# Nystrom attention and two feed-forward layers on one core: GpSimd's subtractions issued in halves

## The chip, the cores and the metric

One core of a Trainium2 chip runs the whole program in one launch. The metric is the device time of that launch in microseconds, the median of several runs. Engines have short names in the profile: PE is TensorE (PEld its weight loads), DVE is VectorE, ACT is ScalarE, POOL is GpSimd, SP is SyncE.

## The reference

Three stages follow each other. Attention with 32 landmarks for 4 batches of 8 heads, 576 positions and 64 channels; a feed-forward layer with the activation h * cos(h); and a second one with a leaky ramp whose slope is learned per channel:

```python
q_lm = q.reshape(B, H, m, S // m, D).mean(axis=3)
k_lm = k.reshape(B, H, m, S // m, D).mean(axis=3)
A, Bm, C = sm(q, k_lm), sm(q_lm, k_lm), sm(q_lm, k)
Z = Bm.transpose(0, 1, 3, 2) / (norm1(Bm) * norminf(Bm) + 1e-06)
for _ in range(6):
    Z = 2 * Z - Z @ Bm @ Z
x = A @ Z @ C @ v                      # to [2304, 512]
h = x @ w_in;  x = (h * np.cos(h)) @ w_out
h = x @ w_in;  out = (np.maximum(h, 0) + alpha * np.minimum(h, 0)) @ w_out
```

`sm` is the scaled softmax. Both layers have 2304 rows, width 512 and inner width 2048. Everything is float32.

## The kernel before, in words

Products in float32 are made of three products in a rounded format. An operand x is split into a high part, `hi = round(x)`, made by ScalarE (`AF.Copy` into a rounded tile), and a low part, `lo = x - hi`, made by a subtraction. A product is then hi*hi + hi*lo + lo*hi, three matmuls into the same PSUM bank. So each operand of each large product passes one subtraction, and the matmuls that read the low part are the last of their three.

The subtractions go through one helper, `sub` (line 413), which issues one `tensor_tensor` on the engine that it is given. Its name stands at line 414 in the profile, whatever it was called for. It is called

- for the low part of a tick's activation, 288 columns (`tick`, L1076 of the source);
- for the low parts of weights and of the second layer's inputs, 256 or 512 columns (`split`, `hl`, `half`, `t_make`, `y_load`), of the attention's rows, 576 columns, and of the second layer's activations (`btick`, `form`);
- for the differences that Strassen's scheme for the second layer needs, 256 columns (`diff_`, `t_make`);
- for subtracting the maximum in the attention's softmax, 18 groups of 32 columns.

The program is recorded first, as operations with their buffers. Then an order written out by hand, the string `ORDER`, says in which order all of them are issued, and where a name ends in `/V` or `/A` also on which engine. An operation that names GpSimd first runs there if the order says nothing else. 200 subtractions run on GpSimd, the others on VectorE. Each engine takes its own instructions in the order in which they are issued; semaphores that are placed by the framework hold an instruction until the data that it reads are written and the buffer that it writes is free. The framework follows this by the range of columns.

Stages, by the profile's time: to about 40 us the attention of the first batch and the conversion of weights; then 128 ticks of the first layer (`tick`) to about 420 us, into which the attention of the other batches is woven; then the second layer (`btick` and, in Strassen's form, `mtick` with `narrow`) to the end. A tick is: six matmuls into a PSUM bank `h` (L1063), a rounding on ScalarE (L1068), a reduction on VectorE that reads PSUM (L1070), a sine on ScalarE (L1072), a product on VectorE that reads PSUM (L1073), the high part on ScalarE (L1075), the low part (L414), and twelve matmuls into four banks `acc` (L1088). Beside the ticks VectorE converts weights with integer operations on 512 columns (L570, L572, L574). L1425 and L1469 are the second layer's first products, L1620 and L1738 its second ones; L409 and L411 copy banks, L1448 and L1481 add them up.

Of the kernel before, what the change touches and what calls it, by code (L numbers as in the profile page):

```python
# [13 lines left out]
ALU = mybir.AluOpType  # L14
# [335 lines left out]
def kernel(  # L350
# [54 lines left out]
    ENG = {"DVE": nc.vector, "POOL": nc.gpsimd}  # L405
# [5 lines left out]
            ENG[e].tensor_copy(o, i)  # L411

    def sub(e, o, a, b):
        ENG[e].tensor_tensor(o, a, b, op=ALU.subtract)  # L414

    ps = ctx.enter_context(tc.tile_pool(name="ps", bufs=2, space=bass.MemoryType.PSUM))
    dram = ctx.enter_context(tc.tile_pool(name="dram", bufs=1, space=bass.MemoryType.DRAM))
# [66 lines left out]
    op = g.op  # L484
# [68 lines left out]
    def split(f, sl, n, hi, lo, target=None, after=(), vec=True):  # L553
        op(act(n), lambda e: nc.scalar.activation(hi.t[:, 0:n], sl(f.t), AF.Copy), r=[f], w=[hi, lo], target=target,
           after=after)
        op([pool(n), dve(n)] if vec else pool(n),
           lambda e: sub(e, lo.t[:, 0:n], sl(f.t), f32(hi.t[:, 0:n])), r=[f, hi], w=[lo], target=target)
# [68 lines left out]
    def unit(u, tu, ta=None):  # L626
# [231 lines left out]
        for ch in range(2):  # L858
# [5 lines left out]
            if m == 0 and ch == 0:  # L864
# [3 lines left out]
               r=[sa[ch]], w=[at])  # L868
        op(dve(S), lambda e, mxa=mxa, at=at: nc.vector.reduce_max(mxa.t, at.t, axis=AX.X), r=[at], w=[mxa])
        op(tt, lambda e, mxa=mxa, at=at: sub(e, at.t, at.t, mxa.t.to_broadcast([P, NBK, M])), r=[mxa], rw=[at])  # L870
        op(act(S), lambda e, at=at: nc.scalar.activation(at.t, at.t, AF.Exp), rw=[at], aset="exp")
        op(dve(S), lambda e, sma=sma, at=at: nc.vector.reduce_sum(sma.t, at.t, axis=AX.X), r=[at], w=[sma])
# [174 lines left out]
    def tick(s):  # L1047
# [9 lines left out]
        def h1_mm(e):  # L1057
# [16 lines left out]
           target=T + 2.6)  # L1074
        op(act(CW), lambda e: nc.scalar.activation(gh.t, hc.t, AF.Copy), r=[hc], w=[gh, gl])  # L1075
        op([pool(CW), dve(CW)], lambda e: sub(e, gl.t, hc.t, f32(gh.t)), r=[hc, gh], w=[gl])  # L1076
        jg = JG if b < 2 else NF
        ja, jb = j // jg * jg, j // jg * jg + jg - 1
# [730 lines left out]
```

## Time and profile before

| | us |
|---|---|
| runs, median (lowest to highest) | 798.35 (797.6 to 801.91) |
| profiled execution, its own time | 795.35 |
| span of its instructions | 793.5 |
| TensorE busy | 776.8 |
| VectorE busy | 640.2 |
| ScalarE busy | 437.6 |
| GpSimd busy | 240.0 |

The span runs from the first to the last instruction; 1.85 us of the execution's time lie around it. Busy time is the union of an engine's instructions; the granted clock is the share of TensorE's 2.4 GHz that the chip gave. A row of a timeline gives start, length, engine, line, operation, what is written from what, how many instructions it merges, and in brackets the idle time of the engine before it and who ended it. Where several instructions are merged, the length is that of all.

### The profile page before, as it was taken

The numbers are of one execution on the slowest core, as the hardware profiler recorded it, in microseconds if no ns is written. First come the engines' busy times: TensorE is split into PE (matmuls) and PEld (weight loads), VectorE is DVE, ScalarE is ACT, GpSimd is POOL, SyncE is SP. The second block draws the span as 40 slices with busy tenths as digits, with TensorE's granted clock in tenths as the row PEclk, the third lists the DMA queues.
The fourth block names the chain that finished last, engine by engine and source line by source line (L and its number), as shares of the span: only waits on it lengthen the run. The fifth ranks groups of instructions, "written<-read, shape, count | busy, mean of one in ns | idle before, by whom it ended". The sixth has DMA issues, their size and how long they took to land. (4 is left out here: it accounts for less than half of the span.)

```text
span 793.5 us, 18121 instructions
## 1 busy us (share of the span) xinstructions
PE 776.8 (98%) x6906; PEld 714.2 (90%) x6906; DVE 640.2 (81%) x1374; ACT 437.6 (55%) x992; POOL 240.0 (30%) x257
## 2 busy tenths in 40 slices
PE   8989999999999999999999999999999999999997
PEld 6577899998988999999998898889889999999997
DVE  4999988788988879888669797676977689776886
ACT  5487666778765555666755343233455475555431
POOL 0334232777323222343534342145311011000200
PEclk9999999999999999999999999999999999999999
DMA  9993447998877657774567854767166514563450
GB/s 284 246 301 129 123 148 170 195 213 175 267 238 250 221 161 261 243 246 135 202 202 269 290 172 158 239 238 266 43 202 227 208 68 139 181 207 125 136 197 28
DMA packets 114278, 154.80 MB, mean 195 GB/s; under 512 B 55568, under 2 KB 73488, under 8 KB 114192
## 3 DMA queue, kind: packets, MB, share of 16 engines
q1 hardware_dynamic: 114032, 153.39, 62.8%
q8 instruction: 54, 0.88, 0.5%
q14 instruction: 32, 0.26, 0.1%
q10 hardware_dynamic: 160, 0.26, 0.1%
HBM read 114.57 MB, written 39.06 MB: 194 GB/s over the span
## 5 line engine op out<-in xcount | busy, mean ns | idle before, releaser
L414 POOL TENSOR_TENSOR m<-m,m 128x288 fp32r<-128x288 f32 (+4 forms) x176 | 176.2, 1014 | 441.3 <-ACT m L1075 138.5
L1088 PE MATMUL acc<-m,m 128*128 128x288 f32 x1536 | 230.9, 298 | 0.0
L1088 PEld LDWEIGHTS acc<-m,m 128*128 128x128 f32 x1536 | 210.6, 188 | 15.3 <-issue 11.9
L414 DVE TENSOR_TENSOR m<-m,m 128x512 fp32r<-128x512 f32 (+5 forms) x268 | 151.9, 587 | 26.5 <-ACT m L1573 12.3
L1063 PE MATMUL h<-m,m 128*128 128x288 f32 x768 | 124.2, 299 | 1.2 <-DVE m L1073 0.7
L1063 PEld LDWEIGHTS h<-m,m 128*128 128x128 f32 x768 | 107.6, 188 | 6.6 <-DVE m L1073 3.8
L1738 PE MATMUL acc<-m,m 128*128 128x512 f32 x384 | 97.3, 394 | 0.0
L1072 ACT ACTIVATE m<-m,quarter 128x288 f32<-128x288 f32 x128 | 67.8, 535 | 44.1 <-DVE m L1070 43.2
L1469 PE MATMUL x<-m,m 128*128 128x256 f32 x588 | 85.6, 286 | 1.8 <-DVE m L414 0.8
L1469 PEld LDWEIGHTS x<-m,m 128*128 128x128 f32 x588 | 75.4, 189 | 4.7 <-ACT m L409 1.4
L1738 PEld LDWEIGHTS acc<-m,m 128*128 128x128 f32 x384 | 68.6, 188 | 11.9
L1073 DVE TENSOR_TENSOR m<-m,h 128x288 f32<-128x288 f32 x128 | 57.0, 449 | 25.6 <-ACT m L1072 20.4
L1573 ACT ACTIVATE m<-m 128x256 fp32r<-128x256 f32 (+2 forms) x96 | 45.8, 508 | 54.1 <-DVE m L1587 21.7
L1068 ACT ACTIVATE m<-h 128x288 int32<-128x288 f32 x128 | 51.5, 404 | 34.5 <-PE h L1063 32.7
L1070 DVE SCALAR_TENSOR_TENSOR m<-h,m 128x288 f32<-128x288 f32 x128 | 57.5, 450 | 15.6 <-ACT m L1068 14.6
L1075 ACT ACTIVATE m<-m 128x288 fp32r<-128x288 f32 x128 | 55.3, 439 | 26.4 <-DVE m L1073 19.8
L1620 PE MATMUL acc<-m,m 128*128 128x256 f32 x485 | 69.0, 281 | 0.1
L1620 PEld LDWEIGHTS acc<-m,m 128*128 128x128 f32 x485 | 62.3, 189 | 0.5 <-ACT m L1573 0.3
L409 ACT ACTIVATE m<-x 128x256 f32<-128x256 f32 (+5 forms) x75 | 29.3, 398 | 38.4 <-PE x L1469 28.6
L574 DVE SCALAR_TENSOR_TENSOR m<-m,m 128x512 int32<-128x512 int32 x64 | 46.7, 734 | 0.3
L572 DVE SCALAR_TENSOR_TENSOR m<-m,m 128x512 int32<-128x512 int32 x64 | 45.3, 711 | 0.3
L1425 PE MATMUL h<-m,m 128*128 128x256 f32 x300 | 43.0, 283 | 0.8 <-ACT m L409 0.8
(176 smaller groups left out, 1121.7 us busy)
## 6 DMA issues: line engine op xcount, KB each, us to landing
m<-wf2d SPq DMA_DIRECT2D x72, 512.0 KB, 4.7
m<-in_moe_w_in_dram SPq DMA_DIRECT2D x32, 512.0 KB, 5.3
m<-in_moe_w_out_dram SPq DMA_DIRECT2D x32, 512.0 KB, 5.5
wf2d<-m SPq DMA_DIRECT2D x28, 512.0 KB, 4.7
m<-w1d SPq DMA_DIRECT2D x32, 256.0 KB, 5.2
m<-wo2d SPq DMA_DIRECT2D x32, 256.0 KB, 3.3
y1d<-m SPq DMA_DIRECT2D x24, 288.0 KB, 4.7
m<-wi2d SPq DMA_DIRECT2D x20, 256.0 KB, 3.8
```

Of the source, the lines that this page charges most:

```text
L414: ENG[e].tensor_tensor(o, a, b, op=ALU.subtract)
L574: op(dve(512), lambda e: nc.vector.scalar_tensor_tensor(cf.t, rv(0), 29, cf.t, op0=ALU.logical_shift_right, op1=ALU.bitwise_or), r=[raw], ...
L1063: nc.tensor.matmul(out=hp.t[:, 0:CW], lhsT=w_[:, js], rhs=x[:, cs], start=(i == 0), stop=(i == 5))
L1068: op(act(CW, True), lambda e: nc.scalar.activation(k_.t, hp.t[:, 0:CW], AF.Copy, scale=INV2PI, bias=0.25), r=[hp], w=[k_], target=T + 0.8)
L1070: op(dve(CW), lambda e: nc.vector.scalar_tensor_tensor(u.t, hp.t[:, 0:CW], INV2PI, k_.t, op0=ALU.mult, op1=ALU.subtract), r=[hp, k_], w=[u])
L1072: op(act(CW), lambda e: nc.scalar.activation(u.t, u.t, AF.Sin, scale=2.0 * math.pi, bias=quarter), rw=[u], aset="sin")
L1073: op(dve(CW), lambda e: nc.vector.tensor_tensor(hc.t, u.t, hp.t[:, 0:CW], op=ALU.mult), r=[hp, u], w=[hc], target=T + 2.6)
L1075: op(act(CW), lambda e: nc.scalar.activation(gh.t, hc.t, AF.Copy), r=[hc], w=[gh, gl])
L1088: nc.tensor.matmul(out=yg[o].t[:, 0:CW], lhsT=w_.t[:, sl], rhs=x.t, start=(j == ja and i == 0), stop=(j == jb and i == 2),)
L1469: nc.tensor.matmul(out=rv(r), lhsT=a_.t[:, p, c2, js], rhs=b_.t[:, q_, c2], start=(first and c2 == 0 and y == 0), stop=(c2 == 1 and y == 2 ...
L1620: nc.tensor.matmul(out=yb.t[:, 256 * (p + yh):256 * (p + yh) + 256], lhsT=a_, rhs=b_, start=(st and p + yh + y == 0), stop=(en and y == 2) ...
L1738: nc.tensor.matmul(out=ya[n][t].t, lhsT=gv(x_), rhs=r_.t, start=(st and k == 0), stop=(en and k == 2))
```

## The change

`sub` issues two instructions where the engine is GpSimd, one for each half of the columns of the last dimension: 576 columns become 288 and 288, 512 become 256 and 256, 288 become 144 and 144, 256 become 128 and 128, and the softmax's groups of 32 become 16 and 16. On VectorE nothing changes.

```diff
     def sub(e, o, a, b):
-        ENG[e].tensor_tensor(o, a, b, op=ALU.subtract)
+        n, parts = o.shape[-1], 2 if e == "POOL" else 1
+        lead = (slice(None),) * (len(o.shape) - 1)
+        for y in range(parts):
+            at_ = (*lead, slice(n * y // parts, n * (y + 1) // parts))
+            ENG[e].tensor_tensor(o[at_], a[at_], b[at_], op=ALU.subtract)
```

Lines behind it stand four further down in the changed kernel (L414 is L418, L1425 is L1429). `ORDER` is the same, and on the other engines the instructions stand as before; the numbers behind the names of tiles only count what was made before them. On GpSimd, at the low parts of the second layer's first weights (about 420 us), the order was this, with the engines that each instruction waits for:

```order
L414 TENSOR_TENSOR m_5055<-m_230,m_5055 128x512 [waits DMAHW1_49,DVE_49,DMAHW3_49,PE_49,Activation_49]
L414 TENSOR_TENSOR m_5055<-m_1328,m_5055 128x512 [waits DMAHW6_49,DMAHW2_49,Activation_49]
L414 TENSOR_TENSOR m_820<-m_274,m_820 128x512 [waits Activation_49]
L414 TENSOR_TENSOR m_1722<-m_1374,m_1721 128x512 [waits DMAHW1_49]
L414 TENSOR_TENSOR m_4542<-m_230,m_4542 128x512 [waits DMAHW5_49,DMAHW4_49,DMAHW7_49,PE_49,Activation_49]
```

and is now

```order
L418 TENSOR_TENSOR m_5159<-m_230,m_5159 128x256 [waits DMAHW1_49,DMAHW3_49,DVE_49,Activation_49]
L418 TENSOR_TENSOR m_5159<-m_230,m_5159 128x256 [waits PE_49]
L418 TENSOR_TENSOR m_5159<-m_1344,m_5159 128x256 [waits DMAHW6_49,DMAHW2_49,Activation_49]
L418 TENSOR_TENSOR m_5159<-m_1344,m_5159 128x256
L418 TENSOR_TENSOR m_827<-m_274,m_827 128x256 [waits Activation_49]
L418 TENSOR_TENSOR m_827<-m_274,m_827 128x256
L418 TENSOR_TENSOR m_1746<-m_1390,m_1745 128x256 [waits DMAHW1_49]
L418 TENSOR_TENSOR m_1746<-m_1390,m_1745 128x256
```

The two halves of a subtraction stand next to each other, nothing comes between them on GpSimd, and the second half waits for nothing of the first. In all GpSimd has 200 instructions more. TensorE has 117 waits for a semaphore of GpSimd before and 133 after; 21 of the 133 are for a first half.

## Rows read from the trace of the kernel before

**Rows 1.** Page, busy time of each engine: us, share of the span, instructions.

```profile
PE 776.8 (98%) x6906; PEld 714.2 (90%) x6906; DVE 640.2 (81%) x1374; ACT 437.6 (55%) x992; POOL 240.0 (30%) x257
```

**Rows 2.** Windows: PE, PEld, DVE, ACT, POOL busy; granted clock, DMA share, GB/s.

```profile
160.00:200.00 40.00, 39.66 (x433) 34.68 (x432) 35.67 (x78) 31.89 (x73) 29.82 (x42) 1.00 0.88 189
```

**Rows 3.** Waits of TensorE's weight loads: releaser, us in total, times, longest.

```profile
PEld h L1063 <- DVE m L1073: 3.8, 9, 0.8
...
PEld x L1469 <- DVE m L1481: 1.8, 5, 0.7
```

**Rows 4.** Line L414 on GpSimd: its groups, and one of those who wait for it.

```profile
L414 POOL TENSOR_TENSOR m<-m,m x176: 731/885/1804, 38.9 to 769.3; 128x288 fp32r<-128x288 f32 x85, 128x512 fp32r<-128x512 f32 x43, 128x256 fp32r<-128x256 f32 x32, 128x256 f32<-128x256 f32 x13
...
  DVE m L1073: 3.5, 5
```

**Rows 5.** GpSimd's groups by form: busy us, mean ns | idle before.

```profile
L759 POOL TENSOR_TENSOR m<-m 128x256 f32<-128x256 f32 x8 | 5.9, 736 | 0.6
...
L759 POOL TENSOR_TENSOR m<-m,m 128x128 f32<-128x128 f32 x8 | 3.7, 460 | 0.6
```

**Rows 6.** Timeline of GpSimd, 441 to 446 us.

```profile
441.65 5.07 POOL L414 TENSOR_TENSOR m<-m,m 128x512 fp32r<-128x512 f32 x4 [2.04 <-ACT m L1211]
```

**Rows 7.** Timeline of all engines around 304 to 305 us.

```profile
304.18 0.45 DVE L1073 TENSOR_TENSOR m<-m,h 128x288 f32<-128x288 f32 x1
304.19 0.81 POOL L414 TENSOR_TENSOR m<-m,m 128x288 fp32r<-128x288 f32 x1 [2.56 <-ACT m L1075]
304.54 0.74 DVE L570 TENSOR_SCALAR m<-m 128x512 int32<-128x512 int32 x1
...
304.71 0.74 PE L1088 MATMUL acc<-m,m 128*128 128x288 f32 x3
```

**Rows 8.** Timeline around 155 us.

```profile
154.37 1.26 POOL L414 TENSOR_TENSOR m<-m,m 128x288 fp32r<-128x288 f32 x1
...
155.37 0.71 PE L1088 MATMUL acc<-m,m 128*128 128x288 f32 x3
```

**Rows 9.** Timeline around 207 us, GpSimd, and TensorE at 208.

```profile
206.85 0.81 POOL L414 TENSOR_TENSOR m<-m,m 128x288 fp32r<-128x288 f32 x1 [4.23 <-ACT m L1075]
...
207.71 0.69 PE L1088 MATMUL acc<-m,m 128*128 128x288 f32 x4
```

**Rows 10.** Timeline, 420 to 425 us.

```profile
420.27 1.38 POOL L414 TENSOR_TENSOR m<-m,m 128x512 fp32r<-128x512 f32 x1 [12.65 <-DMA wf2d<-m]
...
420.42 1.78 DVE L414 TENSOR_TENSOR m<-m,m 128x512 fp32r<-128x512 f32 x1
...
422.91 0.38 ACT L409 ACTIVATE m<-h 128x256 f32<-128x256 f32 x1 [2.20 <-DVE m L1448]
...
423.35 0.98 PE L1425 MATMUL h<-m,m 128*128 128x256 f32 x6 [0.84 <-ACT m L409]
...
424.97 0.68 DVE L414 TENSOR_TENSOR m<-m,m 128x512 fp32r<-128x512 f32 x1
```

**Rows 11.** VectorE's groups by form: busy us, mean ns | idle before.

```profile
L414 DVE TENSOR_TENSOR m<-m,m 128x512 fp32r<-128x512 f32 x109 | 79.8, 745 | 13.1 <-ACT m L1573 5.7 <-ACT m L1726 4.5 <-ACT m L1211 1.2
...
L574 DVE SCALAR_TENSOR_TENSOR m<-m,m 128x512 int32<-128x512 int32 x64 | 46.7, 734 | 0.3
```

**Rows 12.** Timeline, 146 to 150 us.

```profile
146.55 2.80 POOL L414 TENSOR_TENSOR m<-m,m 128x288 fp32r<-128x288 f32 x3
...
147.67 0.96 DVE L1365 TENSOR_SCALAR minus<-alpha_sb 128x16 f32<-128x16 f32 x1
...
149.04 0.83 PEld L1063 LDWEIGHTS h<-m,m 128*128 128x128 f32 x6 [0.57 <-DVE m L1073]
```

**Rows 13.** Timeline, 311 to 313 us.

```profile
311.46 0.81 POOL L414 TENSOR_TENSOR m<-m,m 128x288 fp32r<-128x288 f32 x1 [3.42 <-ACT m L1075]
...
311.73 1.09 DVE L574 SCALAR_TENSOR_TENSOR m<-m,m 128x512 int32<-128x512 int32 x1
...
313.23 0.19 PEld L1063 LDWEIGHTS h<-m,m 128*128 128x128 f32 x1 [0.31 <-DVE m L1073]
```

## The prediction

> **What bounds the kernel now.** I read the busy line first. TensorE is busy for 98% of the span, VectorE for 81%, GpSimd for 30% [rows 1]. Then the stretches, of which I show the one where GpSimd is fullest: TensorE 39.66 of 40 us at a granted clock of 1.00, VectorE 35.67, GpSimd 29.82 [rows 2]. So matmuls set the time, and GpSimd has room even there. What the change can move is therefore what TensorE still waits for. The list of waits of its weight loads names VectorE and ScalarE as releasers, L1063 behind VectorE's L1073 (3.8 us in 9 waits) and L1469 behind L1481 (1.8 us in 5) above all [rows 3]; GpSimd ends none of the waits in it. A subtraction on GpSimd thus reaches TensorE in three ways: it ends later than the slack of the matmul that reads it, it holds back VectorE, or it holds back ScalarE.
>
> **What is added: 200 instructions.** GpSimd's first group of L414 has 176 instructions, one per subtraction [rows 4], and a second one 24; each becomes two, and nothing else on any engine changes place. The price of one more instruction comes from the small forms: 128 columns take 460 ns, 256 take 736 [rows 5]. From 128 to 256 columns 276 ns are added (2.16 a column), which leaves 460 - 276 = 0.18 us that does not depend on the columns. Instructions that follow each other without a wait overlap a little: four of 512 columns stand in 5.07 us [rows 6]; the last of them by itself is 0.18 + 512 x 2.16 ns = 1.29, so one starts (5.07 - 1.29) / 3 = 1.26 us after the other. The real price is then about 0.18 - (1.29 - 1.26) = 0.15 us, and 200 x 0.15 = 30 us of GpSimd's time (240 to 270 us, 34% of the span). No half waits for its own other half, so no semaphore is added between them. The Trainium skill (Perfetto Trace Analysis, "GPSIMD Engine Instruction") says that GpSimd's reported spans are not to be trusted and that the spacing of starts is what counts. The row of four agrees in direction: by durations the sum would be 200 x 0.18 = 36 us, by spacings 30.
>
> Of these 30 us nearly all lies beside matmuls. The cover is the slack between a subtraction's end and the matmul that reads the low part. The tightest place is the subtraction at 304.19: it ends at 305.00, and the third of the three matmuls of L1088 in its row, which read the low part, begins at about 305.05 [rows 7]. The one at 154.37 ends at 155.63 and the last matmul of its row begins at about 155.7 [rows 8]; one more like it stands at 235.4. Going through the 117 places where TensorE waits for a semaphore of GpSimd, I find these 3 with no slack to speak of, 12 below 0.45 us (first the one at 304.19, last the one at 206.85, which ends at 207.66 with its matmul at about 208.1 [rows 7, 9]) and 25 below 0.75 us. Only 21 of the 117 come to wait for the first half alone, and of the three tight ones none does. With 0.15 us more, the three places cost 0.4 us, the nine others next to nothing.
>
> **What is moved: the turn with VectorE.** The price has a second part. At 304.54 VectorE's L570, whose input and output are both in SBUF, takes 0.74 us and ends 0.28 us after the subtraction; L1073, which reads PSUM, runs in 0.45 us beside the same subtraction [rows 7]. At 420.42 a VectorE subtraction takes 1.78 us, not 0.68, because it began 0.15 us into one of GpSimd's that lasts 1.38 [rows 10]. The other way round, the subtraction of 288 columns at 154.37 takes 1.26 us, not 0.81 as at 304.19: VectorE's turn comes first [rows 7, 8]. So the two take turns, an instruction at a time, and halves make the turns shorter. The Trainium skill (SBUF — State Buffer, "Who interferes with whom") calls this an exclusive lock for the whole instruction between GpSimd and a VectorE operation with two SBUF inputs or in a two-port mode. The rows agree, to the point that VectorE ends a fixed time after GpSimd (0.28 and 0.55 us).
>
> For VectorE this is a gain: it waits for a half and not for a whole. Its groups show how much is at stake: L414 with 512 columns has a mean of 745 ns against 0.68 us undisturbed, 109 x 0.065 = 7 us; L574 734 against 0.68, 64 x 0.05 = 3 us [rows 11]. With the groups of like kind beside them I estimate 25 to 30 us, and half of it would go. TensorE sees three places of it. At 423.35 it stands still for 0.84 us behind a copy on ScalarE that waited 2.20 us for VectorE's L1448, queued behind the subtraction of 420.42 [rows 10]. With halves VectorE gets its turn about 0.65 us earlier: -0.65 us. At 149.04 its weight load waits 0.57 us for L1073, which is behind L1365, 0.96 us long for 16 columns, as it meets the second of three subtractions on GpSimd, one of 512 columns [rows 12]: I take -0.45. At 313.23 it waits 0.31 us for an L1073 behind an L574 of 1.09 us that meets the subtraction of 311.46 [rows 13]: -0.25. Together about -1.3 us.
>
> For GpSimd it is a loss: VectorE now gets in between two halves of one subtraction. At 304.19 the first half ends at about 304.69 (0.18 + 144 x 2.16 ns), L570 follows to 304.97, and the second half ends at 304.97 + 0.36 = 305.33: +0.33 us instead of +0.15. An interposed operation of 512 columns would add up to 0.55, so the price of a place lies between 0.15 and 0.70 us less its slack. For the three tight places I take 0.33 + 0.2 + 0.2 = 0.7 (nearest to the worked one), for the nine others 0.1 each, 0.9; bounds 0.4 (0.15 for the three) and 2.8 (0.70 less the slack, for all twelve). ScalarE and VectorE also wait for GpSimd in some places (VectorE's L1073 3.5 us in 5 waits [rows 4]); there 0.15 to 0.33 each, 5 x 0.2 = 1 us off TensorE's path, covered by the other PSUM buffer. I put it at 0; without that cover it is +1. The start, where a softmax runs through GpSimd before the first tick, gets longer by one price per subtraction on its chain and shorter where a matmul reads a first half of 288 columns alone: 0, bounds -0.2 and +0.3.
>
> **The sum.** +0.7 + 0.9 - 1.3 = +0.3 us on the profiled execution of 795.35 us (span 793.5 and 1.85 around it): 795.65. The median of the runs is 798.35, 3.0 above that execution; the same +0.3 gives 798.65, say 798.7 us. I state the forecast against the median.
>
> **The rivals.** *Slower: VectorE between the halves everywhere.* If an operation of 512 columns enters most subtractions, each ends 0.70 us later. Over the 25 places with less slack than that, the excess sums to 7.3 us: 805.7 us. It decides (by the 4 us below) from about 0.5 us of delay on average. For it: VectorE is busy 35.67 of 40 us at 160 to 200 [rows 2], so something is often queued. Against: of its operations in a tick two (L1070, L1073) read PSUM and pass beside, and what enters gains that time on VectorE's side. *Faster: VectorE's relief is worth more than three places.* If the waits behind L1073 and L1481 all came from turns taken late, 3.8 + 1.8 us would go [rows 3]: 792.7 us. By the rule of the Trainium skill on the lock (SBUF — State Buffer, "Who interferes with whom"), taken alone, it would go this way, as shorter instructions block for a shorter time; the trace agrees on the blocks, and shows little of their cost at TensorE. Against: before most of these waits stands a plain chain of ScalarE and VectorE with no slow operation in it, and only a few of them lie beside a subtraction on GpSimd. *Nothing at all:* both parts fall into slack and the time is 798.4 us; this lies inside the forecast. That the change is not carried out is out of the question, since the built program holds the 200 instructions.
>
> **How the numbers follow.** Forecast with the third rival 0.77, slower rival 0.14, faster rival 0.09. A measurement of this kernel tells about 0.5% (4 us) from no change; the runs before spread from 797.6 to 801.91 us. The cases lie on either side of that bound, so faster 0.09, same 0.77, slower 0.14. The range holds the sum's bounds (-1.3 - 0.2 + 0.4 = -1.1 and 2.8 + 1 + 0.3 = +4.1), and some of the faster rival: 795.0 to 803.0 us, -3.4 and +4.7 on the median.
>
> **What would show it.** Right: GpSimd at 265 to 285 us busy, halves of 144 columns at 0.50 us and of 256 at 0.74; VectorE's mean of L414 with 512 columns nearer 0.71 than 0.745; TensorE still at 777 us busy; the matmul behind the subtraction of 304.19 some 0.3 us later, the wait at 423.35 shorter by over half. Wrong: halves that cost over 0.6 us each, waits of TensorE for GpSimd that enter its list, or VectorE's total busy time down by over 20 us with a span that follows.

## The result, and the profile after

| | before | after |
|---|---|---|
| runs, median us | 797.37 (20 runs) | 801.14 (20 runs) |
| ratio of after to before | | 1.0057, 95% interval 1.0046 to 1.0068 |
| profiled execution, us | 795.35 | 801.0 |

The changed kernel is slower by 0.57%, some 4.5 us (3.7 to 5.4). Its 801.14 us lie inside the stated range of 795 to 803 us, 2.4 us above the forecast of 798.7. Part of that is luck: the forecast was set against 798.35 us, the median of three runs, and twenty runs put the kernel before at 797.37. As a change, +0.3 us was forecast and +4.5 measured, which is above the +4.1 that the sum's own bounds allowed. The prediction's line between "same" and "slower" was 4 us, so the result leans to the side that it gave 0.14, though the interval reaches over that line.

The first row of after, the page's busy line, answers to [rows 1]. The next two are of the view by form, GpSimd's groups (busy us, mean ns | idle before), and answer to [rows 4, 5].

```profile
PE 780.4 (98%) x6906; PEld 714.2 (89%) x6906; DVE 636.6 (80%) x1374; ACT 438.3 (55%) x992; POOL 280.0 (35%) x457
```

```profile
L418 POOL TENSOR_TENSOR m<-m,m 128x144 fp32r<-128x144 f32 x170 | 92.4, 567 | 154.6 <-ACT m L1079 151.0 <-DVE m L1074 2.8 <-POOL m L418 0.8
L418 POOL TENSOR_TENSOR m<-m,m 128x256 fp32r<-128x256 f32 x86 | 66.9, 803 | 165.2 <-PE x L1473 73.1 <-ACT m L1730 30.3 <-ACT m L1215 28.4
```

The 200 instructions are there (257 become 457), and GpSimd is busy for 40.0 us more, not 30. A tick's subtraction took 74.8 / 85 = 0.88 us before (85 of 288 columns, 74.8 us in all by the same view) and takes 92.4 / 85 = 1.09 now: 0.21 us more, of which the price of an instruction is some 0.15, and the rest, by the reading of the experiments below, VectorE's turns.

The waits of TensorE's weight loads (releaser, us in total, times, longest), of after. Lines stand four higher than before: L1067 is L1063, L1077 is L1073, L1092 is L1088, L418 is L414.

```profile
PEld h L1067 <- DVE m L1077: 3.5, 9, 0.8
PEld acc L1092 <- POOL m L418: 2.9, 8, 0.6
...
PEld h L792 <- DVE m L1077: 2.7, 5, 0.8
...
PEld x L1473 <- DVE m L1485: 1.4, 5, 0.3
...
PEld x L1473 <- POOL m L418: 0.9, 2, 0.7
```

A releaser is new: GpSimd, 2.9 us in 8 waits, with 0.9 us in 2 more behind L1473. In the list that [rows 3] are from there was none. (TensorE's busy time rose by 3.6 us for the same 6906 matmuls. A matmul of L1092 reads 298 ns on average, but 1536 of them stand in 232.9 us, so one starts 0.15 us after the other while its forerunner still counts as busy. A short pause between starts is therefore hidden in the busy time; the waits of the weight loads show it.) The waits for VectorE hardly fell: L1063's 3.8 became 3.5, L1469's 1.8 became 1.4, and those of L788, 1.5 us in 3 before, are 2.7 in 5.

Where the time is lost is seen by following the same weight loads through both traces. Before, and then after (start, length, engine, line; in brackets the idle time):

```profile
122.99 0.69 PEld L1063 LDWEIGHTS h<-m,m 128*128 128x128 f32 x5 [0.31 <-DVE m L1073]
...
254.31 0.56 PEld L1063 LDWEIGHTS h<-m,m 128*128 128x128 f32 x4 [0.60 <-DVE m L1073]
...
782.52 0.19 PEld L1620 LDWEIGHTS h<-m,m 128*128 128x128 f32 x1 [0.63 <-DVE m L414]
```

```profile
124.06 0.56 PEld L1067 LDWEIGHTS h<-m,m 128*128 128x128 f32 x4 [0.35 <-DVE m L1077]
...
258.16 0.43 PEld L1067 LDWEIGHTS h<-m,m 128*128 128x128 f32 x3 [0.61 <-DVE m L1077]
...
788.19 0.19 PEld L1624 LDWEIGHTS h<-m,m 128*128 128x128 f32 x1 [0.63 <-DVE m L418]
```

They are 1.1, 3.9 and 5.7 us later, and the matmul of 423.35 [rows 10] comes at 428.13, 4.8 us later. So most is lost in the ticks up to 420 us, and 0.9 us behind them. (Some 0.8 us of it was there by 80 us; the start differs by as much between two executions of one kernel, as experiment e7 shows.)

Timelines of after at places that the prediction named: the subtraction of 304.19 [rows 7]; the third subtraction of [rows 12], which before began at 148.56; the matmul of 423.35 [rows 10]; and what comes 20 us behind it.

```profile
308.03 1.14 POOL L418 TENSOR_TENSOR m<-m,m 128x144 fp32r<-128x144 f32 x2 [2.57 <-ACT m L1079]
...
308.39 0.43 DVE L574 TENSOR_SCALAR m<-m 128x512 int32<-128x512 int32 x1
...
309.22 0.69 PEld L1092 LDWEIGHTS acc<-m,m 128*128 128x128 f32 x5 [0.48 <-POOL m L418]
```

```profile
151.24 0.53 PE L1092 MATMUL acc<-m,m 128*128 128x288 f32 x2 [0.21 <-POOL m L418]
```

```profile
428.13 0.98 PE L1429 MATMUL h<-m,m 128*128 128x256 f32 x6 [0.30 <-ACT m L409]
```

```profile
448.58 0.59 PE L1429 MATMUL h<-m,m 128*128 128x256 f32 x3 [0.42 <-ACT m L1730]
```

The first shows the mechanism as it was forecast, to the number: VectorE's integer operation lies between the halves, and the pair lasts 1.14 us where the whole lasted 0.81, +0.33. The second stands 1.3 us behind a place that the prediction took for a gain: the gain came (TensorE's rows of L1088 and L1063 start 1.39 us apart before, at 147.65 and 149.04, and 0.89 us apart after, at 149.04 and 149.93), and TensorE then waits for GpSimd. The third is the gain at 423.35 (0.84 becomes 0.30), the fourth a new wait 20 us later that gives most of it back.

### The profile page after: what moved, and what is told of

It reads as the page before. It is cut to its first block, busy times and chain, and to the rows that moved or that the text cites. A ratio compares the mean times of both kernels' runs of the same rounds, so it can differ in the third digit from the quotient of the medians.

```text
span 799.2 us, 18338 instructions
## 1 busy us (share of the span) xinstructions
PE 780.4 (98%) x6906; PEld 714.2 (89%) x6906; DVE 636.6 (80%) x1374; ACT 438.3 (55%) x992; POOL 280.0 (35%) x457
## 5 line engine op out<-in xcount | busy, mean ns | idle before, releaser
L418 POOL TENSOR_TENSOR m<-m,m 128x144 fp32r<-128x144 f32 (+4 forms) x352 | 210.7, 626 | 412.6 <-ACT m L1079 151.0
L1092 PE MATMUL acc<-m,m 128*128 128x288 f32 x1536 | 232.9, 298 | 1.3 <-POOL m L418 1.0
L1092 PEld LDWEIGHTS acc<-m,m 128*128 128x128 f32 x1536 | 210.8, 188 | 18.6 <-issue 11.9
L418 DVE TENSOR_TENSOR m<-m,m 128x512 fp32r<-128x512 f32 (+5 forms) x268 | 150.0, 579 | 28.6 <-ACT m L1577 12.0
L1067 PE MATMUL h<-m,m 128*128 128x288 f32 x768 | 124.4, 299 | 0.8 <-DVE m L1077 0.6
L1067 PEld LDWEIGHTS h<-m,m 128*128 128x128 f32 x768 | 107.6, 188 | 6.3 <-DVE m L1077 3.5
L1473 PE MATMUL x<-m,m 128*128 128x256 f32 x588 | 86.0, 286 | 1.8 <-DMA m<-wf2d 0.9
L1473 PEld LDWEIGHTS x<-m,m 128*128 128x128 f32 x588 | 75.5, 189 | 4.8 <-DVE m L418 1.1
L1077 DVE TENSOR_TENSOR m<-m,h 128x288 f32<-128x288 f32 x128 | 57.1, 450 | 28.4 <-ACT m L1076 17.4
L418 POOL TENSOR_TENSOR m<-m 128x128 f32<-128x128 f32 (+1 forms) x48 | 28.4, 612 | 50.5 <-DVE m L850 24.4
L578 DVE SCALAR_TENSOR_TENSOR m<-m,m 128x512 int32<-128x512 int32 x64 | 44.8, 704 | 0.3
L576 DVE SCALAR_TENSOR_TENSOR m<-m,m 128x512 int32<-128x512 int32 x64 | 44.7, 702 | 0.3
```

What stands on the lines that cost most here:

```text
L418: ENG[e].tensor_tensor(o[at_], a[at_], b[at_], op=ALU.subtract)
L1067: nc.tensor.matmul(out=hp.t[:, 0:CW], lhsT=w_[:, js], rhs=x[:, cs], start=(i == 0), stop=(i == 5))
L1077: op(dve(CW), lambda e: nc.vector.tensor_tensor(hc.t, u.t, hp.t[:, 0:CW], op=ALU.mult), r=[hp, u], w=[hc], target=T + 2.6)
L1092: nc.tensor.matmul(out=yg[o].t[:, 0:CW], lhsT=w_.t[:, sl], rhs=x.t, start=(j == ja and i == 0), stop=(j == jb and i == 2),)
L1473: nc.tensor.matmul(out=rv(r), lhsT=a_.t[:, p, c2, js], rhs=b_.t[:, q_, c2], start=(first and c2 == 0 and y == 0), stop=(c2 == 1 and y == 2 ...
```

## The experiments

Each stands against the kernel before, run on the same chip beside it; "+" is the ratio's excess times the median of before (796.1 to 797.0 us). GpSimd's added time is its busy time in the one profile less 240.0 us.

| | what differs from before | time, us (95%) | GpSimd, us |
|---|---|---|---|
| e1 | ticks halved | +2.5 (1.1 to 3.7) | +16.9 |
| e2 | all but the ticks halved | +4.0 (2.2 to 5.7) | +22.5 |
| e3 | ticks cut into 280 + 8 columns | +3.2 (2.2 to 4.3) | +22.1 |
| e4 | ticks cut into 8 + 280 | +2.7 (1.4 to 4.1) | +14.0 |
| e5 | four buffers, subtractions whole | +0.1 (-1.4 to 1.7) | -0.6 |
| e6 | four buffers, all halved | +5.0 (2.9 to 7.1) | +39.9 |
| e7 | 12 tight places halved | +2.9 (1.6 to 4.3) | +2.7 |
| e8 | all but these 12 halved | +3.7 (2.0 to 5.3) | +38.0 |
| e9 | whole, and 200 writes nobody reads | +1.9 (0.8 to 3.0) | +16.7 |
| e10 | low part read last, whole | +1.1 (-0.4 to 2.6) | -0.7 |
| e11 | low part read last, all halved | +5.7 (4.1 to 7.2) | +39.2 |
| e12 | all in quarters | +29.1 (27.1 to 31.0) | +124.4 |
| | the change | +4.5 (3.7 to 5.4) | +40.0 |

**Which subtractions, and which cut (e1 to e4).** The theories of these four: A, VectorE's turn between two parts of a tick's subtraction costs; B, each additional instruction at the ticks costs, however it is cut; C, the loss comes from the subtractions outside the ticks. `cuts` replaces the halves in the helper, with one of the four lines in each kernel:

```diff
-        ENG[e].tensor_tensor(o, a, b, op=ALU.subtract)
+        n, cuts = o.shape[-1], (0, o.shape[-1])
+        if e == "POOL":
+            cuts = (0, n // 2, n) if n == CW else (0, n)    # e1
+            cuts = (0, n) if n == CW else (0, n // 2, n)    # e2
+            cuts = (0, n - 8, n) if n == CW else (0, n)     # e3
+            cuts = (0, 8, n) if n == CW else (0, n)         # e4
+        lead = (slice(None),) * (len(o.shape) - 1)
+        for x, y in zip(cuts, cuts[1:]):
+            at_ = (*lead, slice(x, y))
+            ENG[e].tensor_tensor(o[at_], a[at_], b[at_], op=ALU.subtract)
```

> Only the 85 tick subtractions on GpSimd (288 columns) are halved; the 115 others stay whole. In the trace of the changed kernel the instructions of VectorE are late by 0.8 us at 100 us, by 5.3 us at 415 us and by 5.7 us at the end, so the loss is made in the ticks. Theory A (VectorE takes its turn between the halves and the matmuls that read the low part come late): +4 us against the kernel before (3 to 5.5), with TensorE's waits for GpSimd of about 3 us. Theory B (the fixed price of one more instruction, 0.15 us, closes the slack): the same +4. Theory C (the loss has many places, start and weights too): +2 or less.

> The reverse: the 115 subtractions outside the ticks are halved, the 85 of 288 columns stay whole. Theories A and B: 0 us (-1 to +1), no wait of TensorE for GpSimd in its list during the ticks. Theory C: +2 us or more.

> Only the tick subtractions are cut, into 280 and 8 columns: the same number of instructions and the same fixed price as halves, but nearly every operation of VectorE that arrives during a subtraction arrives in its first part and goes in before the tail, and its own wait is as long as before. Theory A: worse than halves, +5 to +9 us. Theory B: the same as halves, +4 us.

> Only the tick subtractions are cut, into 8 and 280 columns: the same number of instructions and the same fixed price, but an operation of VectorE seldom arrives in the first 0.2 us, so it seldom gets in between. Theory A: +1 us (0 to 2). Theory B: the same as halves, +4 us.

The ticks alone cost +2.5, and e2 refutes A and B: the other 115 subtractions, at which I had seen next to nothing, cost +4.0. C has e2 for it, but the ticks cost too. The two together, 6.5, are above the 4.5 of the change, by less than the intervals allow. Between the cuts the times don't differ by more than their intervals. The profile does see VectorE's turn. GpSimd's groups of 8 columns by form, of e3 and then of e4:

```profile
L420 POOL TENSOR_TENSOR m<-m,m 128x8 fp32r<-128x8 f32 x85 | 28.7, 337 | 0.0
```

```profile
L420 POOL TENSOR_TENSOR m<-m,m 128x8 fp32r<-128x8 f32 x85 | 23.6, 277 | 164.2 <-ACT m L1081 157.3 <-DVE m L1076 2.8 <-PE acc L1094 1.6
```

Eight columns last longer as a tail (337 ns) than as a head (277), and GpSimd is busy for 22.1 us more in e3, 14.0 in e4: in the tail VectorE has often stepped in between. These 8 us of GpSimd's time make 0.5 us of the kernel's (3.2 against 2.7), less than the intervals, where A expected 3 us or more between the two. The turns are there, and A as the main cause falls.

**Is it the wait for a buffer? (e5, e6).** In after, VectorE's product of a tick (L1077) waits 9.5 us in 14 places for GpSimd, where L1073 waited 3.5 in 5 [rows 4]: the buffer that it writes is still read by a subtraction. From here on theory L says that a low part which ends later than its matmul's slack costs the time; Q, that VectorE and ScalarE are held up behind GpSimd and pass it on. The edit lets the product overwrite its input, so that four buffers serve where two and two did:

```diff
-("hc", 2, 4 * CW), ("kk", 2, 4 * CW))
+("kk", 4, 4 * CW))
-hp, k_, u, hc = psb("h"), tk("t", dt=I32), tk("kk"), tk("hc")
+hp, k_, (u, hc) = psb("h"), tk("t", dt=I32), 2 * [tk("kk")]
-...hc.t, u.t, hp.t[:, 0:CW], op=ALU.mult), r=[hp, u], w=[hc],
+...hc.t, u.t, hp.t[:, 0:CW], op=ALU.mult), r=[hp], rw=[u],
```

> The kernel before, with one edit in the ticks: the product of L1073 is written over its own input, and the two pairs of buffers that held input and product become four buffers of one name. VectorE then no longer waits for GpSimd's subtraction of two ticks earlier before it may write a product; no instruction is added. Theory L (what costs in the change is that a low part ends later than the slack of the matmul that reads it): 0 against the kernel before (-1 to +1 us). Theory Q (what costs is VectorE and ScalarE held up behind GpSimd, who pass it on): the 3.5 us in five waits of L1073 for GpSimd go, and the time falls by 1 to 2 us.

> The changed kernel with the same edit of the buffers. In the changed kernel VectorE's product waits 9.5 us in 14 places for GpSimd; these waits go. Theory L: as the changed kernel, +4 us against the kernel before (3 to 5.5). Theory Q: the loss falls to +2.5 us or less.

VectorE's groups by form, of after and then of e6:

```profile
L1077 DVE TENSOR_TENSOR m<-m,h 128x288 f32<-128x288 f32 x128 | 57.1, 450 | 28.4 <-ACT m L1076 17.4 <-POOL m L418 9.5
```

```profile
L1077 DVE TENSOR_TENSOR m<-m,h 128x288 f32<-128x288 f32 x128 | 57.1, 448 | 20.6 <-ACT m L1076 19.9
```

The 9.5 us behind GpSimd are gone from e6, and the loss is still there (+5.0); without halves nothing is gained either (+0.1). Q by way of this buffer is refuted. By way of other buffers, and of ScalarE's waits, no run tried it; the traces show one such way, told in the next section.

**The twelve tight places (e7, e8).** `nth` counts the ticks' subtractions on GpSimd; `TIGHT` holds the twelve that had less than 0.45 us of slack before.

```diff
+    nth, TIGHT = iter(range(128)), (7, 13, 18, 23, 28, 34, 38, 49, 57, 65, 69, 83)
...
+        k = next(nth) if e == "POOL" and n == CW else None
+        parts = 2 if k in TIGHT else 1      # e7
+        parts = 1 if k in TIGHT else 2      # e8, on GpSimd
```

> The kernel before with only 12 of the 200 subtractions halved: the twelve of the ticks whose matmul had less than 0.45 us of slack in the trace of before, those that the prediction counted. Theory L: nearly the whole loss of the 85 ticks, +2 us (1.2 to 3.0; the waits of TensorE for GpSimd at such places sum to 2.3 us in the trace of the changed kernel). Theory Q: twelve of 200 instructions, at most +0.6 us.

> The changed kernel with those twelve subtractions whole, the other 188 halved. Theory L: the loss falls to +2.5 us (1.5 to 3.5) against the kernel before. Theory Q: it stays at +4.3 us (3.5 to 5).

e7 is L's number: 12 of 200 instructions cost +2.9 us (1.6 to 4.3), as much as all 85 of e1. Its profile shows five of the waits, one of them the place of 304.19 again, with the same 1.13 us and 0.48 us of idle time as in after:

```profile
306.91 1.13 POOL L423 TENSOR_TENSOR m<-m,m 128x144 fp32r<-128x144 f32 x2 [2.57 <-ACT m L1084]
...
308.10 0.69 PEld L1097 LDWEIGHTS acc<-m,m 128*128 128x128 f32 x5 [0.48 <-POOL m L423]
```

```profile
PEld acc L1097 <- POOL m L423: 1.7, 5, 0.5
```

The list was therefore right as to where. It wasn't complete: the other 188 cost +3.7, where L expected 1.5 to 3.5 and Q 3.5 to 5. The waits of weight loads in e8:

```profile
PEld h L1072 <- DVE m L1082: 4.6, 11, 0.8
PEld h L797 <- DVE m L1082: 3.2, 5, 0.8
...
PEld acc L1097 <- POOL m L423: 1.4, 5, 0.4
```

Five waits for GpSimd are left in the ticks (1.4 us). Two of them, 0.63 us, are at other places; three, 0.81 us, are at tight places whose own subtraction is whole here (156.49, 238.98 and 308.21). The first of these stands behind a subtraction that is halved. Two more waits for GpSimd, 0.8 us, stand behind L1478 (L1469 before), and the waits for VectorE's product, 3.8 + 1.5 = 5.3 us in 12 before (the first in [rows 3]), are 7.8 in 16. In time, +3.7 (2.0 to 5.3) holds both L's range and Q's, so e8 doesn't decide between them. Each trace is one execution, so a row that no other kernel repeats is no more than a hint. In e7 the weight load at 57.25 us of before comes 1.5 us later, though nothing differs up to 100 us; that much two executions differ at the start.

**Is it enough that GpSimd has more to do? (e9).** Theory N says that any 200 instructions more on GpSimd cost this.

```diff
         ENG[e].tensor_tensor(o, a, b, op=ALU.subtract)
+        if e == "POOL":
+            nc.gpsimd.memset(scrap, 0.0)        # 64 columns
```

> The kernel before with its 200 subtractions whole; behind each, GpSimd writes 64 columns of zeros that nobody reads. It is as many additional instructions on GpSimd as in the change, and 0.1 to 0.2 us each, but no low part waits for its own. Theory L (what costs is that a low part ends later than the slack of the matmul that reads it): only subtractions that start right behind another GpSimd instruction end later (five of the twelve tight places do), so +0.5 us against the kernel before (-0.5 to +1.5). Theory N (any 200 more instructions on GpSimd cost this, through its queue or otherwise): +4 us (3 to 5.5).

```profile
L416 POOL MEMSET scrap<- 128x64 f32 x200 | 30.6, 153 | 0.0
```

```profile
154.06 1.06 POOL L414 TENSOR_TENSOR m<-m,m 128x288 fp32r<-128x288 f32 x1 [1.15 <-ACT m L1078]
...
155.17 1.17 POOL L414 TENSOR_TENSOR m<-m,m 128x288 fp32r<-128x288 f32 x1
...
156.38 0.70 PEld L1091 LDWEIGHTS acc<-m,m 128*128 128x128 f32 x5 [0.23 <-POOL m L414]
```

```profile
PEld acc L1091 <- POOL m L414: 0.4, 2, 0.2
```

(Of e9: GpSimd's group by form, rows of the timeline, and the waits of weight loads.) The write costs 153 ns by its row, but part of it overlaps the subtractions beside it, and GpSimd's busy time grows by 16.7 us only. The time grows by 1.9 us (0.8 to 3.0), between L and N. Per microsecond of GpSimd's time that is 1.9 / 16.7 = 0.11, and in the change 4.5 / 40.0 = 0.11; that the two agree is no rule, as e7 has 2.9 / 2.7. The weight load of the matmul that had no slack [rows 8] waits 0.23 us for GpSimd (156.38), but the write is not seen to be the cause: the two subtractions ahead of it last 2.28 us from start to end, as before (154.06 to 156.34 here, 153.35 to 155.63 before), and ScalarE releases the first of them 0.71 us later. TensorE's waits for GpSimd are but 0.4 us, so nearly all of the 1.9 comes by a way that I can't name.

**Reading the low part later (e10, e11).**

```diff
-for i, (w_, x) in enumerate(((wh, gh), (wh, gl), (wl, gh))):
+for i, (w_, x) in enumerate(((wh, gh), (wl, gh), (wh, gl))):
```

> The kernel before, the subtractions whole; of the three matmuls that L1088 issues for each bank, the one that reads the low part of the activation comes third and no longer second, so it starts 0.13 us later in each tick. Theory L: three places without slack gain little, 0 to -0.5 us against the kernel before. Theory N: 0.

> The changed kernel with the same order of the three matmuls. Theory L: the twelve tight places gain 0.13 us of slack each, about 1.2 us of the loss; +3 us against the kernel before (2 to 4). Theory N: as the changed kernel, +4.5 us.

Of a bank's three matmuls in a tick, the low part of the activation is read by the second and that of the weight by the third; the edit swaps these two. Where L expected e10 to gain 0 to 0.5 us, no gain is seen (+1.1, -0.4 to 2.6). The waits of weight loads of e11:

```profile
PEld h L1067 <- DVE m L1077: 4.0, 10, 0.8
...
PEld acc L1092 <- POOL m L418: 1.5, 5, 0.4
```

The waits for GpSimd fall from 2.9 us in 8 to 1.5 in 5, as L said, by 1.4 us; but the time doesn't fall with them (+5.7 against +4.5, intervals that overlap). So a wait that is taken from TensorE at one place in the ticks isn't simply gained: here the waits for VectorE's product are larger (3.5 to 4.0). As a forecast of time L failed.

**The dose (e12).**

```diff
-n, parts = o.shape[-1], 2 if e == "POOL" else 1
+n, parts = o.shape[-1], 4 if e == "POOL" else 1
```

> The changed kernel with four parts in place of two: three additional instructions per subtraction and not one. Theory L: a low part ends later by 0.45 us plus VectorE's turns, and more and more of the 117 places where TensorE waits for GpSimd come to bind, so the loss grows at least in proportion: +10 to +16 us against the kernel before. A rival S (the loss saturates, since a delay of TensorE at one place gives slack to the next): +5 to +8 us.

GpSimd's group by form and the waits of weight loads, of e12; then two windows (PE, PEld, DVE, ACT, POOL busy; granted clock, DMA share, GB/s) and TensorE's timeline there:

```profile
L418 POOL TENSOR_TENSOR m<-m,m 128x72 fp32r<-128x72 f32 x340 | 127.7, 407 | 127.4 <-ACT m L1079 114.9 <-PE h L1067 7.3 <-DVE m L576 4.3
```

```profile
PEld acc L1092 <- POOL m L418: 12.7, 19, 1.5
...
PEld x L1429 <- issue: 3.8, 1, 3.8
```

```profile
552.00:555.40 3.40, 0.00 (x0) 0.00 (x0) 1.80 (x2) 0.48 (x2) 3.40 (x8) 1.00 0.51 186
...
557.00:559.00 2.00, 2.00 (x8) 1.71 (x8) 0.00 (x0) 0.00 (x0) 0.00 (x0) 0.51 0.37 131
```

```profile
551.00 0.87 PE L1429 MATMUL h<-m,m 128*128 128x256 f32 x6
555.44 1.52 PE L1429 MATMUL x<-m,m 128*128 128x256 f32 x6 [3.57 <-DMA m<-wf2d]
```

A tick's subtraction now takes 127.7 / 85 = 1.50 us, 0.62 more than whole, three times the 0.21 of halves. The time grows by 29 us, over six times the 4.5. Both L in proportion (10 to 16) and saturation (5 to 8) fall: the cost rises faster than the delay. The waits for GpSimd in the ticks go from 2.9 us in 8 to 12.7 in 19, as more places use up their slack. Some 4.5 us come from a single place: from 550.40 GpSimd works through 16 quarters in a row (5.93 us), TensorE waits 3.57 us for a transfer of `wf2d` (0.73 at the same matmul before, at 530.13), and the next six matmuls take 1.52 us where six like them took 0.87 at 551.00, as the granted clock is down to 0.55 and 0.51 until 559 (1.6 x 0.45 + 2.0 x 0.49 = 1.7 us lost). How that transfer hangs on the quarters I didn't follow.

## Why the prediction was right or wrong

The range held and the mechanism that was named, VectorE's turn between two halves, is there; but the sum was too low by more than its bounds, since it put at nothing the places that aren't on the list of tight ones. Of the signs named beforehand, GpSimd's 280 us, the matmul behind 304.19 and the wait at 423.35 came out as forecast. The means of the halves, VectorE's mean and TensorE's busy time (780.4 us, not 777) did not, and one sign of being wrong came out: GpSimd has entered the list of TensorE's waits.

- **The price of one more instruction, 0.15 us: right.** The four subtractions of 512 columns of [rows 6] took 5.07 us and take 5.60 as eight halves, (5.60 - 5.07) / 4 = 0.13 each:

```profile
447.04 5.60 POOL L418 TENSOR_TENSOR m<-m,m 128x256 fp32r<-128x256 f32 x8 [2.04 <-ACT m L1215]
```

- **GpSimd's total: too low.** 280 us is within the 265 to 285 named, but 10 above the 270 worked out: VectorE's turns, on average 0.05 us a subtraction, that were priced at single places and left out of the total. The halves' means (567 and 803 ns against 0.50 and 0.74) hold the same.
- **VectorE's relief: half right.** By form, L578 (L574 before) fell from 734 to 704 ns, and the subtractions of 512 columns stayed at 740 against 745 [rows 11], where 0.71 was expected:

```profile
L418 DVE TENSOR_TENSOR m<-m,m 128x512 fp32r<-128x512 f32 x109 | 79.2, 740 | 13.7 <-ACT m L1577 5.7 <-ACT m L1730 5.3 <-ACT m L1215 1.0
...
L578 DVE SCALAR_TENSOR_TENSOR m<-m,m 128x512 int32<-128x512 int32 x64 | 44.8, 704 | 0.3
```

  VectorE's busy time fell by 3.6 us, not by half of 25 to 30. An operation of VectorE still meets one half after the other: beside the four halves of 438.73 (3.73 us) two of its operations take 1.20 and 1.23 us, where 0.69 is usual; beside the two wholes of 433.18 (3.45 us) it was 1.01 and 1.78.
- **The turns themselves: right.** The Trainium skill (SBUF — State Buffer, "Who interferes with whom") has GpSimd and a VectorE operation with two SBUF inputs or in a two-port mode exclude each other for a whole instruction; the 0.33 us at 308.03 and the 337 against 277 ns of e3 and e4 agree.
- **The tight places, +0.7 and +0.9: too low, but inside their bounds.** They were found in the right spots (e7), and at 304.19 the price was met. In the trace of after six of the twelve have a wait for GpSimd in the list (104.52, 157.69, 239.78, 309.22, 340.15 and 355.44), together 2.2 us where the sum had 1.6.
- **The places with more slack, put at nothing: the step that failed.** The other four waits for GpSimd come to 1.5 us: 151.24 (0.44), 366.04 (0.21), 664.92 (0.18) and 666.39 (0.69). I set the price of one instruction against a slack that one trace showed, while a subtraction that stands behind others inherits their delays. The subtraction of 148.56 had 0.72 us of slack and is the third of a row. That of 666.39 is the third of three that took 2.77 us from 656.89 and take 4.01 us from 662.32, as six halves: 1.24 us more, against 0.6 of slack (its matmul ran at 660.27).

```profile
666.39 0.50 PE L1473 MATMUL x<-m,m 128*128 128x256 f32 x2 [0.49 <-POOL m L418]
```

  This place repeats. From the matmuls of L1620 that start at 657.00 to those that start at 660.60 it is 3.60 us before, 4.57 to 4.59 in the five kernels that halve the subtractions outside the ticks (after, e2, e6, e8, e11), and 3.57 or 3.58 in the other seven (e12 aside).
- **The relief of TensorE, -1.3: right at its three places.** At 423.35 the wait fell by 0.54 (0.65 forecast), at 149.04 by 0.50 (0.45) and at 313.23 by 0.24 (0.25). What the sum lacked is the waits that came instead.
- **What waits for GpSimd without being a matmul, put at 0: it failed too, and in part stays open.** For the buffer of the product 0 was right (e6). For another buffer it was not: VectorE's L1721 (L1725 after) writes a buffer that GpSimd has not yet freed. Its releaser is a subtraction, and the subtractions that run there write low parts, which L1721 doesn't read. Before, after, and e2:

```profile
437.11 0.47 DVE L1721 TENSOR_SCALAR m<-m,alpha_sb 128x512 f32<-128x512 f32 x1
...
443.21 0.92 PE L1425 MATMUL h<-m,m 128*128 128x256 f32 x6
```

```profile
442.49 0.49 DVE L1725 TENSOR_SCALAR m<-m,alpha_sb 128x512 f32<-128x512 f32 x1 [0.63 <-POOL m L418]
```

```profile
442.71 0.49 DVE L1727 TENSOR_SCALAR m<-m,alpha_sb 128x512 f32<-128x512 f32 x1 [1.33 <-POOL m L420]
...
448.80 0.95 PE L1431 MATMUL h<-m,m 128*128 128x256 f32 x6 [1.60 <-ACT m L1732]
```

  The chain behind it in after (VectorE's and GpSimd's L1249, VectorE's L1728, ScalarE's L1730, the matmul of 448.58) keeps its length, 6.1 us from 437.11 to 443.21 before and from 442.49 to 448.58 after, so what VectorE waits for GpSimd TensorE waits too. From the matmul of L1738 at 439.74 to that of 443.21 it is 3.47 us before, 3.47 or 3.48 in the seven kernels without such halves, and 4.06 to 5.24 in the five with them: 0.6 us in the change, 1.8 in e2, 1.3 in e8. This, with the place at 666.39, is a part of why e2 and e8 cost what they do with few waits of TensorE for GpSimd itself.

  Of the 5.3 us by which the pair of profiled executions differs from the sum (5.65 against 0.3), 0.6 are the twelve tight places, 1.5 the other waits for GpSimd, 0.6 this chain and some 0.8 the start. What is left, about 2 us, and nearly all of e9, reaches TensorE by ways that these runs don't separate. The waits of L788 for VectorE's product (1.5 to 2.7 us) are a part of it; some of it is what two executions differ by.
- **The start, 0:** within what two executions differ by.
- **The rivals.** The slower one asked for an average delay of 0.5 us and priced it at 7.3 us over 25 places. In the ticks the average was 0.21; but at 0.62 (e12) the loss was 29 us, some 24.6 without the place at 555 us, so its price from the slack of one trace was too low by a factor of three. The faster one is out: the two waits for VectorE went from 3.8 + 1.8 to 3.5 + 1.4 us.

No variant here beats the kernel before.

## What to carry to other kernels

When an engine that isn't the bottleneck gets slower by a fixed amount per instruction, don't add up only the places whose slack is below that amount: its own queue adds the amounts up, and a slack read from one trace is itself the outcome of waits that move. Take such a list as where the loss will begin, not as its sum (here the waits for that engine came to over twice that), look for buffers that it frees for another engine, and expect that the loss can grow faster than the delay. Shorter instructions give the other engine earlier turns, but a low part that is read late pays for these turns.

## What was not expected of the hardware

- A write of 64 columns on GpSimd behind a subtraction reads 153 ns but adds only 16.7 us / 200 = 0.08 us to GpSimd's busy time: an instruction's reported span overlaps the next one's (in e9 the subtraction of 155.17 ends at 156.34 by its row, and the write behind it begins at 156.28).
- In e12 the granted clock was 1.00 through 3.57 us without a matmul, and 0.51 in the window from 557 to 559 us, with TensorE busy throughout; by the 559 to 560 window it was 1.00 again:

```profile
559.00:560.00 1.00, 1.00 (x10) 1.00 (x10) 0.15 (x1) 0.56 (x2) 0.00 (x0) 1.00 0.00 0
```

  0.51 is the lower level of 1.2 GHz, so the wait cost half its length again.
